# A decode block on one core: ScalarE's softmax work as a hardware loop, and one row of w_down per partition loaded ahead in three transfers

## The chip, the core and the metric

The kernel runs on one core of a Trainium2 chip. The metric is the device time of one execution in microseconds; before the change its median is 409.87 us over three runs (409.83 to 410.06). The profile shows one execution with its engines: PE (matmuls; its weight loads are shown as PEld), DVE (VectorE), ACT (ScalarE), POOL (GpSimd) and SP, which here only issues transfers. Behind SP's queue sixteen DMA engines move the bytes.

## What is computed

One token (B = S = 1) goes through an attention block over a cache of 65,536 keys and then through a gated feed-forward block. Everything is bf16 at the interface.

```python
D = 1024; Hq, Hkv, Sk, Dh = 32, 4, 65536, 128; F = 3584
q = (layernorm(x) @ wq).reshape(B, Sq, Hq, Dh).transpose(0, 2, 1, 3)
k, v = repeat(k_cache, 8, axis=1), repeat(v_cache, 8, axis=1)
p = softmax(einsum("bhqd,bhkd->bhqk", q, k) * Dh ** -0.5)
h = x + einsum("bhqk,bhkd->bhqd", p, v).transpose(0, 2, 1, 3).reshape(B, Sq, Hq * Dh) @ wo
n = layernorm(h)
h2 = h + (gelu(n @ w_gate) * (n @ w_up)) @ w_down
```

The caches are 2 x 64 MiB, the weights wq and wo 8 MiB each, w_gate, w_up and w_down 7 MiB each: 173 MB in all, every byte read once.

## The kernel before

**Staging.** All large inputs go through one buffer, `ring` (L162), of four slots of 32 KB per partition (4 MiB each). wq is read into slots 0 and 1. Then the caches are read in *half heads*: each of the four K/V heads is cut into two halves of 32,768 keys, so that `NT2` = 8 half heads t = 0 to 7 are worked on, one after the other. Of each, K comes as two transfers of 4 MiB, one to slot 2 and one to slot 3 (`k_load`, L211), and V as one of 8 MiB to slots 0 and 1 (`v_load`, L217). Behind the last half head wo takes slots 2 and 3, w_gate slots 0 and 1, w_up slots 2 and 3, and w_down slots 0 and 1 again.

**One half head.** DVE transposes K in four chunks (`k_chunk`), PE multiplies them with the query (L427), DVE transposes the scores into `sc` (`score`) and takes maxima. `softmax(t)` (L377) makes the maximum common to all partitions with two small PE operations and writes the negative bias `nb`. ACT then makes eight exponentials, one per query head, from `sc` into `pt`, each with a row sum into `lp` (L386). PE multiplies `pt` with V in 64 matmuls (L439), ACT copies the sum out of PSUM into `acc_sb` (`acc_copy`, L391), PE folds it with eight more (L448), and DVE copies the result to `o_raw` (`o_copy`).

**Who orders it.** The class `Flow` (L17) holds a list of operations for all engines; `op` (L31) finds which earlier operation each must wait for, and `issue` (L76) writes them out engine by engine in the order of the list, with semaphore waits. PE's part of the eight half heads alone is a hardware loop (`pe_loop`, L415), placed with `loop` (L66); ACT's and DVE's parts are written out eight times. PE counts its steps of a half head on the semaphore `s_step`, `STEPS` = 5 for each: 1 the transpose of the maxima, 2 the broadcast of the bias, 3 the first matmul with V, 4 the last matmul with V, 5 the last of the folding matmuls. Waits on this count are: `v_load(t)` on step 4 of half head t - 1, `score(t, 0)` on step 3 of t - 1, `softmax(t)` on steps 1 and 2, `acc_copy(t)` on step 4, `o_copy(t)` on step 5, and the load of w_gate on step 4 of half head 7 (L536).

**SP's queue** is served in order: wq twice, K(0) twice, then for each t V(t) and the two loads of K(t+1), then wo (L503), w_gate and w_up (L536), and w_down (L580 to L585) in four transfers.

**w_down.** Each partition gets 28 rows of 1,024 numbers (2 KB). The first 16 (`wa`, `FA` = 16) go to slot 0 as one transfer; the other 12 (`wb`, `FB` = 12) to slot 1 as three transfers of 8, 3 and 1 rows, each with its semaphore. At the end, outside the list, PE waits for each of these parts in turn and multiplies its rows (`down`, L590), eight matmuls a row, with some filling matmuls before the first and the second part (`stay_busy`, L596). DVE and ACT then copy the two halves of the result to `h2` (L607, L608), and SP stores it (L609).

**The end of the attention** (L454 to L478): from the biases DVE makes `mn` and `df`, ACT the factors `fa` that bring the two halves of a head to one scale, DVE the sums `lw` and `lsum`, PE adds them over partitions, and DVE weights `o_raw` with them. wo follows, then the second layer norm, w_gate, w_up and w_down.

Of the kernel before, what the change touches and what calls it, by code (L numbers as in the profile page):

```python
# [16 lines left out]
class Flow:  # L17
# [45 lines left out]
            self.readers[k] = []  # L63
        self.ops.append(dict(e=e, call=call, kw=kw, deps=sorted(deps), wait=wait, inc=inc, dma=dma))

    def loop(self, body):  # L66
        self.ops.append(dict(e="pe", call=body, loop=True, dma=False, inc=None))

    def dma(self, e, out, in_, r=(), w=(), after=(), wait=(), inc=None, sem=None):
        self.op(e, "dma_start", r, w, after, wait, inc, True, out=out, in_=in_)  # L70
# [38 lines left out]
def kernel(  # L109
# [76 lines left out]
    f = Flow(nc, tc)  # L186
    op = f.op
    from_dve, from_act, from_pool, s_v = [tc.alloc_semaphore("to_pe_%d" % i) for i in range(4)]
    s_qk, s_step = [tc.alloc_semaphore("from_pe_%d" % i) for i in range(2)]
    STEPS = 5  # L190
    k_sem = [tc.alloc_semaphore("k_landed_%d" % i) for i in range(DCH)]
    r_sem = [tc.alloc_semaphore("r_landed_%d" % i) for i in range(3)]

# [23 lines left out]
    def v_load(t):  # L217
        g, h = divmod(t, NH)
        n0 = h * CPH * CH
        f.dma("sp", slot(0, 2).rearrange("p (n d) -> p n d", d=Dh), v_v[g][:, n0:n0 + CPH * CH, :], after=["R0", "R1"],  # L220
              wait=[(s_step, STEPS * t - 1)] if t else [], inc=(s_v, 16))

    for p in range(PPH):
        k_load(0, p)
# [138 lines left out]

    def score(t, c):
        n = t * CPH + c
        op("dve", "transpose", w=["sc%d" % c], wait=[(s_qk, n + 1)] + ([(s_step, STEPS * t - 2)] if t and c == 0 else []),
           out=sc[:, c].rearrange("p n h s -> p (n h s)"), in_=bank[n % 2][:])
        if c >= CPH - 2:
            c0, i = (0, 0) if c == CPH - 2 else (c, 1)
            op("dve", "tensor_reduce", r=["sc%d" % x for x in range(c0, c + 1)], w=["mx%d" % i], out=mx[:, i, :],  # L370
               in_=sc[:, c0:c + 1].rearrange("p c n h s -> p h (c n) s"), axis=AX.XY, op=ALU.max)

    def o_copy(t):
        g, h = divmod(t, NH)
        op("dve", "tensor_copy", w=["o_raw%d" % t], wait=[(s_step, STEPS * t + 5)], out=o_raw[:, g, h, :], in_=o_ps)

    def softmax(t):  # L377
        g, h = divmod(t, NH)
        op("dve", "tensor_tensor", r=["mx0", "mx1"], inc=(from_dve, 1), out=mx1[:], in0=mx[:, 0, :], in1=mx[:, 1, :], op=ALU.max)
        op("dve", "tensor_reduce", w=["gm"], wait=[(s_step, STEPS * t + 1)], out=gm[:], in_=mxT_ps, axis=AX.X, op=ALU.max)  # L380
        op("dve", "tensor_scalar", r=["gm", "ident_f"], inc=(from_dve, 1), out=diag[:], in0=ident_f[0:rep, 0:rep], scalar1=gm[:, 0:1], scalar2=None,
           op0=ALU.mult)
        op("dve", "tensor_scalar", w=["nb%d" % t], wait=[(s_step, STEPS * t + 2)], out=nb[:, g, h, :], in0=bc_ps, scalar1=-scale, scalar2=None, op0=ALU.mult)
        for r in range(rep):
            last = r == rep - 1
            op("act", "activation", r=["nb%d" % t] if r == 0 else [], w=[] if last else ["lp%d_%d" % (t, r)],  # L386
               inc=(from_act, 1) if last else None,
               out=pt[:].rearrange("p c n h s -> p (c n) h s")[:, :, r, :], in_=sc[:].rearrange("p c n h s -> p (c n) h s")[:, :, r, :],
               func=ACT.Exp, bias=nb[:, g, h, r:r + 1], scale=scale, accum_out=lp[:, g, h, r:r + 1])

    def acc_copy(t):  # L391
        op("act", "copy", wait=[(s_step, STEPS * t + 4)], inc=(from_act, 1), out=acc_sb[:], in_=acc[:])

    for t in range(NT2):
        if t % NH == 0:
            make_qs(t // NH)
        for c in range(CPH):
            k_chunk(t, c)
            if c >= 1:
                score(t, c - 1)  # L400
            elif t:
                o_copy(t - 1)
        score(t, CPH - 1)
        v_load(t)
        if t + 1 < NT2:
            for p in range(PPH):
                k_load(t + 1, p)
        softmax(t)
        if t + 1 < NT2:
            acc_copy(t)  # L410

    def take(sem, n=1):
        nc.tensor.wait_ge(sem, n).then_inc(sem, -n)  # L413
# [1 line left out]
    def pe_loop():  # L415
        v_sb = slot(0, 2).rearrange("p (c s n d) -> p c s n d", c=CPH, s=NS, d=Dh)
        with nc.Fori(0, NT2, engines=(mybir.EngineType.PE,), head_slot={mybir.EngineType.PE: 0}):
            take(from_pool)
            with nc.tensor.Fori(0, PPH):
                for c in range(DCH):  # L420
                    take(from_dve)
                    for s in range(NS):
                        mv = ktb[:, c, s, :].bitcast(BF16).rearrange("p (n j b t) -> p n j b t", n=NN, j=2, t=2)
                        for jt in range(4):
                            J, u = divmod(jt, 2)
                            last = (s, jt) == (NS - 1, 3)
                            m = nc.tensor.matmul(bank[c][:], lhsT=qs[:, jt].rearrange("p s c -> p (s c)")[:, s * P:(s + 1) * P], rhs=mv[:, :, J, :, u], start=(s == 0 and jt == 0), stop=last)  # L427
                            if last:
                                m.then_inc(s_qk, 1)
            take(from_dve)  # L430
            nc.tensor.transpose(out=mxT_ps, in_=mx1[:], identity=ident_f[:]).then_inc(s_step, 1)  # L431
            take(from_dve)
            nc.tensor.matmul(bc_ps, lhsT=ones_f[0:rep, :], rhs=diag[:], start=True, stop=True).then_inc(s_step, 1)  # L433
            take(from_act)
            take(s_v, 16)
            for c in range(CPH):
                for n in range(NN):
                    q = n % 4
                    m = nc.tensor.matmul(acc[32 * q:32 * q + 32, :], lhsT=pt[:, c, n, :, :].rearrange("p h s -> p (h s)"),  # L439
                                         rhs=v_sb[:, c, :, n, :], start=(c == 0 and n < 4), stop=(c == CPH - 1 and n >= NN - 4),  # L440
                                         tile_position=(0, 32 * q))
                    if (c, n) == (0, 0):
                        m.then_inc(s_step, 1)
                    if (c, n) == (CPH - 1, NN - 1):
                        m.then_inc(s_step, 1)
            take(from_act)
            for u in range(NS):
                m = nc.tensor.matmul(o_ps, lhsT=acc_sb[:, u * Dh:(u + 1) * Dh], rhs=sel[:, u:SQ:NS], start=(u == 0), stop=(u == NS - 1))  # L448
            m.then_inc(s_step, 1)
# [5 lines left out]
    mn = sb("mn", [P, Hkv, rep])  # L455
    df = sb("df", [P, Hkv, NH, rep])
    fa = sb("fa", [P, Hkv, NH, rep])
    op("dve", "tensor_tensor", r=keys("nb"), w=["mn"], out=mn[:], in0=nb[:, :, 0, :], in1=nb[:, :, 1, :], op=ALU.min)
    for h in range(NH):
        op("dve", "tensor_tensor", r=["mn"], w=["df%d" % h], out=df[:, :, h, :], in0=mn[:], in1=nb[:, :, h, :], op=ALU.subtract)  # L460
    op("act", "activation", r=["df0", "df1"], w=["fa"], out=fa[:], in_=df[:], func=ACT.Exp)
# [1 line left out]
    op("dve", "tensor_tensor", r=["fa"], w=["lw"], out=lw[:], in0=lp[:], in1=fa[:], op=ALU.mult)  # L463
    lsum = sb("lsum", [P, Hkv, rep])
    op("dve", "tensor_tensor", r=["lw"], w=["lsum"], out=lsum[:], in0=lw[:, :, 0, :], in1=lw[:, :, 1, :], op=ALU.add)
    acc_copy(NT2 - 1)
    l_ps = bank[4][:, 0:Hq]
    op("pe", "matmul", r=["lsum", "ones_f"], w=["B4"], out=l_ps, lhsT=ones_f[:], rhs=lsum[:].rearrange("p g r -> p (g r)"), start=True, stop=True)
    rl = sb("rl", [P, Hkv, rep])
# [31 lines left out]
    at_ps = bank[6][:]  # L501
    wv = slot(2, 2).rearrange("p (c n) -> p c n", c=Hq)
    f.dma("sp", wv, A_wo.rearrange("(p c) n -> p c n", p=P), w=["R2", "R3"], wait=done, sem=r_sem[2])  # L503
    for c in range(Hq):
        for s in range(DS):
            q = 2 * (c % 2) + s
            op("pe", "matmul", r=["o2z", "R2", "R3"], w=["B6"], out=at_ps[32 * q:32 * q + 32, :], lhsT=o2z[:, c, :],
               rhs=wv[:, c, :].rearrange("k (p s c) -> k s p c", s=DS, c=C4)[:, s], start=(c < 2), stop=(c >= Hq - 2), tile_position=(0, 32 * q))
# [22 lines left out]
    def ffn_in(wmat, key, s0, b0):  # L531
# [1 line left out]
        bkeys = ["B%d" % (b0 + i) for i in range(2)]  # L533
        rk = ["R%d" % s0, "R%d" % (s0 + 1)]
        wv = slot(s0, 2)[:, 0:DC * F].rearrange("p (c n) -> p c n", c=DC)
        f.dma("sp", wv, wmat.rearrange("(p c) n -> p c n", p=P), w=rk, sem=r_sem[s0], wait=[(s_step, STEPS * NT2 - 1)])  # L536
        for ci in range(DC):
            wide_rows(banks, bkeys, hz, "xz", ci, f_blocks(wv[:, ci, :]), rk, ci == 0, ci == DC - 1)
        return rows_to_columns(banks, bkeys, key, "p (j e) -> p e j", j=32)
# [36 lines left out]
    FZ = 4  # L576
    wa = slot(0)[:, 0:FA * D].rearrange("p (e n) -> p e n", e=FA)
    wb = slot(1)[:, 0:FB * D].rearrange("p (e n) -> p e n", e=FB)
    wb_src = B_w_down[P * FA:F, :].rearrange("(p e) n -> p e n", p=P)
    parts = [(wa, 0, FA, f.dma("sp", wa, B_w_down[0:P * FA, :].rearrange("(p e) n -> p e n", p=P), after=["R0"], inc=(r_sem[0], 16)), r_sem[0])]  # L580
    e0 = 0
    for i, z in enumerate((FB - FZ, FZ - 1, 1)):
        part = wb[:, e0:e0 + z, :]
        s = (r_sem[1], k_sem[0], k_sem[1])[i]
        parts.append((part, FA + e0, z, f.dma("sp", part, wb_src[:, e0:e0 + z, :], after=["R1"] if i == 0 else [], inc=(s, 16)), s))  # L585
        e0 += z
# [12 lines left out]

    with tc.tile_critical(no_gpsimd_drain=True):  # L600
        for w_rows, a0, n, at, sem in parts:
            stay_busy({0: 4, FA: 4}.get(a0, 0))
            nc.tensor.wait_ge(sem, at)
            for e in range(n):
                down(actz[:, a0 + e, :], w_rows[:, e, :])
    h2 = sb("h2", [P, 2, OB], BF16)
# [33 lines left out]
```

## Time and profile before

| what | us |
|---|---|
| median of three runs | 409.87 |
| the profiled execution, its own time | 409.71 |
| its span | 407.8 |
| busy: PE / DVE / ACT / POOL | 234.8 / 202.5 / 39.5 / 19.2 |
| transfers of SP's queue, share of 16 engines' span | 98.5% |
| bytes read | 173.02 MB |
| one exponential on ACT / the eight of a half head | 0.49 / 3.9 |
| a copy to `acc_sb` on ACT | 0.59 |

The span runs from the first to the last thing that the profile shows; the profiled execution's own time is 1.9 us more. No engine but the transfers is busy for more than 58% of the span. ACT stands idle for 255.3 us in front of the exponentials, waiting for `nb`.

Two more kinds of record lie in the trace. Each transfer raises its semaphore in several events, one for each DMA engine as it finishes its share: they give the time at which each of the sixteen lands, though not which engine it is. And instructions are fetched by the same DMA engines, in blocks: five of 16 KB on queue 8, at 33.22, 358.00, 376.88, 401.08 and 404.62 us, and two of 8 KB on queue 14, at 99.83 and 143.25 us, in the span up to the last load.

### The profile page before, as it was taken

The numbers are of one execution on the slowest core, as the hardware profiler recorded it, in microseconds if no ns is written. First come the engines' busy times: TensorE is split into PE (matmuls) and PEld (weight loads), VectorE is DVE, ScalarE is ACT, GpSimd is POOL, SyncE is SP. The second block draws the span as 40 slices with busy tenths as digits, with TensorE's granted clock in tenths as the row PEclk, the third lists the DMA queues.
The fourth block names the chain that finished last, engine by engine and source line by source line (L and its number), as shares of the span: only waits on it lengthen the run. The fifth ranks groups of instructions, "written<-read, shape, count | busy, mean of one in ns | idle before, by whom it ended". The sixth has DMA issues, their size and how long they took to land. (4 is left out here: it accounts for less than half of the span.)

```text
span 407.8 us, 3909 instructions
## 1 busy us (share of the span) xinstructions
PE 234.8 (58%) x1645; PEld 105.8 (26%) x1647; DVE 202.5 (50%) x174; ACT 39.5 (10%) x141; POOL 19.2 (5%) x39
## 2 busy tenths in 40 slices
PE   0433855585577368734973686557465747365376
PEld 0211322232232133212321232223132223142324
DVE  1218860876089328924781687089508941010210
ACT  1000003000300300030003000300220021000000
POOL 4210000001000000010000001000000000012000
PEclk9955995599569967978796689689976976565668
DMA  8999999999999999999998999999999999999995
GB/s 344 427 421 452 415 460 411 460 418 412 453 460 418 411 425 488 418 408 421 476 437 376 453 424 444 421 460 418 411 453 466 418 418 424 452 440 435 399 413 220
DMA packets 4815, 173.12 MB, mean 424 GB/s; under 512 B 580, under 2 KB 584, under 8 KB 840
## 3 DMA queue, kind: packets, MB, share of 16 engines
q1 hardware_dynamic: 4760, 173.02, 98.5%
q8 instruction: 5, 0.08, 0.1%
q14 instruction: 2, 0.02, 0.0%
q10 hardware_dynamic: 48, 0.00, 0.0%
HBM read 173.02 MB, written 0.00 MB: 424 GB/s over the span
## 5 line engine op out<-in xcount | busy, mean ns | idle before, releaser
L95 DVE STREAM_TRANSPOSE ktb<-ring 128x4096 f32<-128x4096 f32 x32 | 141.1, 4418 | 83.4 <-DMA ring<-in_A_k_cache_dram 83.4
L427 PE MATMUL bank<-ktb,qs 128*128 128x512 bf16 x512 | 132.6, 418 | 61.3 <-PEq L413 61.3
L427 PEld LDWEIGHTS bank<-ktb,qs 128*128 128x128 bf16 x512 | 51.5, 104 | 139.2 <-issue 93.6
L439 PE MATMUL bank<-ring,pt 128*32 128x512 bf16 x512 | 46.3, 541 | 36.5 <-PEq L413 36.5
L95 ACT ACTIVATE pt<-sc,nb 128x256 bf16<-128x256 f32 x64 | 31.5, 494 | 255.3 <-DVE nb L95 255.3
L439 PEld LDWEIGHTS bank<-ring,pt 128*32 128x32 bf16 x512 | 19.4, 131 | 60.2 <-issue 57.3
L95 DVE STREAM_TRANSPOSE sc<-bank 128x512 f32<-128x512 f32 x32 | 22.2, 695 | 24.6 <-PE bank L427 24.6
L95 PE MATMUL bank<-ring,xz 128*32 128x512 bf16 (+1 forms) x192 | 19.2, 587 | 17.2 <-DMA ring<-in_B_w_gate_dram 5.2
L95 DVE TENSOR_REDUCE mx<-sc 128x8 f32<-128x1536 f32 (+1 forms) x16 | 19.5, 1219 | 0.5
L95 DVE STREAM_TRANSPOSE ktb<-bank 128x512 f32<-128x512 f32 (+1 forms) x6 | 4.0, 672 | 31.3 <-PE bank L95 30.9
L95 POOL COPY qs<-qsel 32x128 bf16<-32x128 bf16 x16 | 7.8, 490 | 231.4 <-PE bank L427 216.8
L95 PEld LDWEIGHTS bank<-ring,xz 128*32 128x32 bf16 x192 | 7.5, 141 | 26.9 <-issue 15.9
L95 ACT ACTIVATION_READ_ACCUMULATOR pt<-sc,nb 128x1 f32 x64 | 12.0, 187 | 0.0
L448 PE MATMUL bank<-sel,acc_sb 128*128 128x8 f32 x64 | 8.2, 255 | 6.2 <-PEq L413 6.2
L431 PE MATMUL bank<-ident_f,mx 128*8 128x128 f32 x8 | 2.2, 269 | 14.6 <-PEq L413 14.6
L448 PEld LDWEIGHTS bank<-sel,acc_sb 128*128 128x128 f32 x64 | 7.7, 191 | 10.0 <-issue 10.0
L95 PE MATMUL bank<-ring,ktb 128*32 128x512 bf16 x64 | 6.4, 586 | 5.9 <-DMA ring<-in_A_wo_dram 5.9
L95 ACT COPY acc_sb<-bank 128x512 f32<-128x512 f32 x8 | 4.7, 586 | 48.9 <-PE bank L439 48.9
L95 DVE TENSOR_TENSOR h_col<-bank,x_col 128x8 f32<-128x8 f32 x1 | 0.2, 167 | 14.8 <-PE bank L95 14.8
L95 PE MATMUL bank<-sel,ktb 128*128 128x16 f32 (+1 forms) x24 | 5.2, 356 | 3.5 <-DVE bank L95 2.7
L95 POOL MEMSET ktb<- 128x1024 bf16 (+2 forms) x3 | 3.5, 1164 | 75.8 <-PE bank L427 75.8
L433 PE MATMUL bank<-diag,ones_f 8*128 8x8 f32 x16 | 3.7, 299 | 5.7 <-PEq L413 5.7
(85 smaller groups left out, 60.9 us busy)
## 6 DMA issues: line engine op xcount, KB each, us to landing
ring<-in_A_k_cache_dram SPq DMA_DIRECT2D x16, 4096.0 KB, 24.9
ring<-in_A_wq_dram SPq DMA_DIRECT2D x2, 4096.0 KB, 16.7
ring<-in_B_w_gate_dram SPq DMA_DIRECT2D x1, 7168.0 KB, 26.9
ring<-in_B_w_up_dram SPq DMA_DIRECT2D x1, 7168.0 KB, 27.2
ring<-in_B_w_down_dram SPq DMA_DIRECT2D x1, 4096.0 KB, 20.4
ring<-in_B_w_down_dram SPq DMA_DIRECT2D x1, 2048.0 KB, 25.0
ring<-in_B_w_down_dram SPq DMA_DIRECT2D x1, 768.0 KB, 25.9
ring<-in_B_w_down_dram SPq DMA_DIRECT2D x1, 256.0 KB, 26.0
```

What stands on the lines that cost most here:

```text
L95: ins = getattr(self.eng[e], o["call"])(**o["kw"])
L427: m = nc.tensor.matmul(bank[c][:], lhsT=qs[:, jt].rearrange("p s c -> p (s c)")[:, s * P:(s + 1) * P], rhs=mv[:, :, J, :, u], start=(s == ...
L431: nc.tensor.transpose(out=mxT_ps, in_=mx1[:], identity=ident_f[:]).then_inc(s_step, 1)
L433: nc.tensor.matmul(bc_ps, lhsT=ones_f[0:rep, :], rhs=diag[:], start=True, stop=True).then_inc(s_step, 1)
L439: m = nc.tensor.matmul(acc[32 * q:32 * q + 32, :], lhsT=pt[:, c, n, :, :].rearrange("p h s -> p (h s)"), rhs=v_sb[:, c, :, n, :], start=(c ...
L448: m = nc.tensor.matmul(o_ps, lhsT=acc_sb[:, u * Dh:(u + 1) * Dh], rhs=sel[:, u:SQ:NS], start=(u == 0), stop=(u == NS - 1))
```

## The change

ACT's eight copies of exponentials and copy become one hardware loop over the half heads, `act_loop`. It is started for each half head by a semaphore of its own, `act_go`, which `softmax` raises when `nb` is written, and takes the count back by one each time. The operands `nb` and `lp` of a half head are addressed with the loop's register. For the copy to `acc_sb`, PE now raises a semaphore of its own too, `s_acc`, in place of step 4; so `STEPS` is 4 and step 4 is now the last of the folding matmuls. The loads of V and of w_gate and w_up wait for this step. `mn` waits for step 3 of the last half head. The last `acc_copy`, which stood behind `fa` in ACT's order, is now inside the loop and ahead of it.

The first of the 12 rows of `wb`, 256 KB over the 128 partitions, gets a tile of its own, `c_row`. It is loaded by three transfers, of the partitions 0 to 50, 51 to 114 and 115 to 127, which stand in SP's queue behind wo and ahead of w_gate and wait for nothing. The parts of `wb` behind it have 7, 3 and 1 rows. PE multiplies `c_row` at the head of the part of 7 rows, so the matmuls and their order stay as they were.

```diff
@@ -63,8 +63,8 @@
             self.readers[k] = []
         self.ops.append(dict(e=e, call=call, kw=kw, deps=sorted(deps), wait=wait, inc=inc, dma=dma))
 
-    def loop(self, body):
-        self.ops.append(dict(e="pe", call=body, loop=True, dma=False, inc=None))
+    def loop(self, body, e="pe"):
+        self.ops.append(dict(e=e, call=body, loop=True, dma=False, inc=None))
 
     def dma(self, e, out, in_, r=(), w=(), after=(), wait=(), inc=None, sem=None):
         self.op(e, "dma_start", r, w, after, wait, inc, True, out=out, in_=in_)
@@ -186,8 +186,9 @@
     f = Flow(nc, tc)
     op = f.op
     from_dve, from_act, from_pool, s_v = [tc.alloc_semaphore("to_pe_%d" % i) for i in range(4)]
-    s_qk, s_step = [tc.alloc_semaphore("from_pe_%d" % i) for i in range(2)]
-    STEPS = 5
+    s_qk, s_step, s_acc = [tc.alloc_semaphore("from_pe_%d" % i) for i in range(3)]
+    act_go = tc.alloc_semaphore("to_act")
+    STEPS = 4
     k_sem = [tc.alloc_semaphore("k_landed_%d" % i) for i in range(DCH)]
     r_sem = [tc.alloc_semaphore("r_landed_%d" % i) for i in range(3)]
 
@@ -218,7 +219,7 @@
         g, h = divmod(t, NH)
         n0 = h * CPH * CH
         f.dma("sp", slot(0, 2).rearrange("p (n d) -> p n d", d=Dh), v_v[g][:, n0:n0 + CPH * CH, :], after=["R0", "R1"],
-              wait=[(s_step, STEPS * t - 1)] if t else [], inc=(s_v, 16))
+              wait=[(s_step, STEPS * t)] if t else [], inc=(s_v, 16))
 
     for p in range(PPH):
         k_load(0, p)
@@ -363,7 +364,7 @@
 
     def score(t, c):
         n = t * CPH + c
-        op("dve", "transpose", w=["sc%d" % c], wait=[(s_qk, n + 1)] + ([(s_step, STEPS * t - 2)] if t and c == 0 else []),
+        op("dve", "transpose", w=["sc%d" % c], wait=[(s_qk, n + 1)] + ([(s_step, STEPS * t - 1)] if t and c == 0 else []),
            out=sc[:, c].rearrange("p n h s -> p (n h s)"), in_=bank[n % 2][:])
         if c >= CPH - 2:
             c0, i = (0, 0) if c == CPH - 2 else (c, 1)
@@ -372,7 +373,7 @@
 
     def o_copy(t):
         g, h = divmod(t, NH)
-        op("dve", "tensor_copy", w=["o_raw%d" % t], wait=[(s_step, STEPS * t + 5)], out=o_raw[:, g, h, :], in_=o_ps)
+        op("dve", "tensor_copy", w=["o_raw%d" % t], wait=[(s_step, STEPS * t + 4)], out=o_raw[:, g, h, :], in_=o_ps)
 
     def softmax(t):
         g, h = divmod(t, NH)
@@ -380,16 +381,21 @@
         op("dve", "tensor_reduce", w=["gm"], wait=[(s_step, STEPS * t + 1)], out=gm[:], in_=mxT_ps, axis=AX.X, op=ALU.max)
         op("dve", "tensor_scalar", r=["gm", "ident_f"], inc=(from_dve, 1), out=diag[:], in0=ident_f[0:rep, 0:rep], scalar1=gm[:, 0:1], scalar2=None,
            op0=ALU.mult)
-        op("dve", "tensor_scalar", w=["nb%d" % t], wait=[(s_step, STEPS * t + 2)], out=nb[:, g, h, :], in0=bc_ps, scalar1=-scale, scalar2=None, op0=ALU.mult)
-        for r in range(rep):
-            last = r == rep - 1
-            op("act", "activation", r=["nb%d" % t] if r == 0 else [], w=[] if last else ["lp%d_%d" % (t, r)],
-               inc=(from_act, 1) if last else None,
-               out=pt[:].rearrange("p c n h s -> p (c n) h s")[:, :, r, :], in_=sc[:].rearrange("p c n h s -> p (c n) h s")[:, :, r, :],
-               func=ACT.Exp, bias=nb[:, g, h, r:r + 1], scale=scale, accum_out=lp[:, g, h, r:r + 1])
-
-    def acc_copy(t):
-        op("act", "copy", wait=[(s_step, STEPS * t + 4)], inc=(from_act, 1), out=acc_sb[:], in_=acc[:])
+        op("dve", "tensor_scalar", wait=[(s_step, STEPS * t + 2)], inc=(act_go, 1), out=nb[:, g, h, :], in0=bc_ps, scalar1=-scale, scalar2=None, op0=ALU.mult)
+
+    def act_loop():
+        with nc.scalar.Fori(0, NT2) as t:
+            nc.scalar.wait_ge(act_go, 1).then_inc(act_go, -1)
+            nb_t = nb[:].rearrange("p g h r -> p (g h) r")[:, bass.ds(t, 1), :].rearrange("p t r -> p (t r)")
+            lp_t = lp[:].rearrange("p g h r -> p (g h) r")[:, bass.ds(t, 1), :].rearrange("p t r -> p (t r)")
+            for r in range(rep):
+                m = nc.scalar.activation(out=pt[:].rearrange("p c n h s -> p (c n) h s")[:, :, r, :], in_=sc[:].rearrange("p c n h s -> p (c n) h s")[:, :, r, :],
+                                         func=ACT.Exp, bias=nb_t[:, r:r + 1], scale=scale, accum_out=lp_t[:, r:r + 1])
+            m.then_inc(from_act, 1)
+            nc.scalar.wait_ge(s_acc, 1).then_inc(s_acc, -1)
+            nc.scalar.copy(out=acc_sb[:], in_=acc[:]).then_inc(from_act, 1)
+
+    f.loop(act_loop, "act")
 
     for t in range(NT2):
         if t % NH == 0:
@@ -406,8 +412,6 @@
             for p in range(PPH):
                 k_load(t + 1, p)
         softmax(t)
-        if t + 1 < NT2:
-            acc_copy(t)
 
     def take(sem, n=1):
         nc.tensor.wait_ge(sem, n).then_inc(sem, -n)
@@ -442,7 +446,7 @@
                     if (c, n) == (0, 0):
                         m.then_inc(s_step, 1)
                     if (c, n) == (CPH - 1, NN - 1):
-                        m.then_inc(s_step, 1)
+                        m.then_inc(s_acc, 1)
             take(from_act)
             for u in range(NS):
                 m = nc.tensor.matmul(o_ps, lhsT=acc_sb[:, u * Dh:(u + 1) * Dh], rhs=sel[:, u:SQ:NS], start=(u == 0), stop=(u == NS - 1))
@@ -455,7 +459,7 @@
     mn = sb("mn", [P, Hkv, rep])
     df = sb("df", [P, Hkv, NH, rep])
     fa = sb("fa", [P, Hkv, NH, rep])
-    op("dve", "tensor_tensor", r=keys("nb"), w=["mn"], out=mn[:], in0=nb[:, :, 0, :], in1=nb[:, :, 1, :], op=ALU.min)
+    op("dve", "tensor_tensor", w=["mn"], wait=[(s_step, STEPS * NT2 - 1)], out=mn[:], in0=nb[:, :, 0, :], in1=nb[:, :, 1, :], op=ALU.min)
     for h in range(NH):
         op("dve", "tensor_tensor", r=["mn"], w=["df%d" % h], out=df[:, :, h, :], in0=mn[:], in1=nb[:, :, h, :], op=ALU.subtract)
     op("act", "activation", r=["df0", "df1"], w=["fa"], out=fa[:], in_=df[:], func=ACT.Exp)
@@ -463,7 +467,6 @@
     op("dve", "tensor_tensor", r=["fa"], w=["lw"], out=lw[:], in0=lp[:], in1=fa[:], op=ALU.mult)
     lsum = sb("lsum", [P, Hkv, rep])
     op("dve", "tensor_tensor", r=["lw"], w=["lsum"], out=lsum[:], in0=lw[:, :, 0, :], in1=lw[:, :, 1, :], op=ALU.add)
-    acc_copy(NT2 - 1)
     l_ps = bank[4][:, 0:Hq]
     op("pe", "matmul", r=["lsum", "ones_f"], w=["B4"], out=l_ps, lhsT=ones_f[:], rhs=lsum[:].rearrange("p g r -> p (g r)"), start=True, stop=True)
     rl = sb("rl", [P, Hkv, rep])
@@ -501,6 +504,10 @@
     at_ps = bank[6][:]
     wv = slot(2, 2).rearrange("p (c n) -> p c n", c=Hq)
     f.dma("sp", wv, A_wo.rearrange("(p c) n -> p c n", p=P), w=["R2", "R3"], wait=done, sem=r_sem[2])
+    wb_src = B_w_down[P * FA:F, :].rearrange("(p e) n -> p e n", p=P)
+    c_row = sb("c_row", [P, 1, D], BF16)
+    for p0, p1 in ((0, 51), (51, 115), (115, P)):
+        f.dma("sp", c_row[p0:p1], wb_src[p0:p1, 0:1, :], inc=(r_sem[1], 16))
     for c in range(Hq):
         for s in range(DS):
             q = 2 * (c % 2) + s
@@ -533,7 +540,7 @@
         bkeys = ["B%d" % (b0 + i) for i in range(2)]
         rk = ["R%d" % s0, "R%d" % (s0 + 1)]
         wv = slot(s0, 2)[:, 0:DC * F].rearrange("p (c n) -> p c n", c=DC)
-        f.dma("sp", wv, wmat.rearrange("(p c) n -> p c n", p=P), w=rk, sem=r_sem[s0], wait=[(s_step, STEPS * NT2 - 1)])
+        f.dma("sp", wv, wmat.rearrange("(p c) n -> p c n", p=P), w=rk, sem=r_sem[s0], wait=[(s_step, STEPS * NT2)])
         for ci in range(DC):
             wide_rows(banks, bkeys, hz, "xz", ci, f_blocks(wv[:, ci, :]), rk, ci == 0, ci == DC - 1)
         return rows_to_columns(banks, bkeys, key, "p (j e) -> p e j", j=32)
@@ -576,10 +583,9 @@
     FZ = 4
     wa = slot(0)[:, 0:FA * D].rearrange("p (e n) -> p e n", e=FA)
     wb = slot(1)[:, 0:FB * D].rearrange("p (e n) -> p e n", e=FB)
-    wb_src = B_w_down[P * FA:F, :].rearrange("(p e) n -> p e n", p=P)
     parts = [(wa, 0, FA, f.dma("sp", wa, B_w_down[0:P * FA, :].rearrange("(p e) n -> p e n", p=P), after=["R0"], inc=(r_sem[0], 16)), r_sem[0])]
-    e0 = 0
-    for i, z in enumerate((FB - FZ, FZ - 1, 1)):
+    e0 = 1
+    for i, z in enumerate((FB - FZ - 1, FZ - 1, 1)):
         part = wb[:, e0:e0 + z, :]
         s = (r_sem[1], k_sem[0], k_sem[1])[i]
         parts.append((part, FA + e0, z, f.dma("sp", part, wb_src[:, e0:e0 + z, :], after=["R1"] if i == 0 else [], inc=(s, 16)), s))
@@ -599,8 +605,10 @@
 
     with tc.tile_critical(no_gpsimd_drain=True):
         for w_rows, a0, n, at, sem in parts:
-            stay_busy({0: 4, FA: 4}.get(a0, 0))
+            stay_busy({0: 4, FA + 1: 4}.get(a0, 0))
             nc.tensor.wait_ge(sem, at)
+            if a0 == FA + 1:
+                down(actz[:, FA, :], c_row[:, 0, :])
             for e in range(n):
                 down(actz[:, a0 + e, :], w_rows[:, e, :])
     h2 = sb("h2", [P, 2, OB], BF16)

```

## Prediction

> **What bounds the kernel.** I read the page's slices and queues first, then the chain of waits, then the timeline around the places that the change touches. The slices and queues:
>
> ```profile
> PE   0433855585577368734973686557465747365376
> DVE  1218860876089328924781687089508941010210
> DMA  8999999999999999999998999999999999999995
> ...
> q1 hardware_dynamic: 4760, 173.02, 98.5%
> q8 instruction: 5, 0.08, 0.1%
> q14 instruction: 2, 0.02, 0.0%
> ...
> HBM read 173.02 MB, written 0.00 MB: 424 GB/s over the span
> ```
>
> The DMA row is full from the second slice to the last but one, while PE and DVE have holes everywhere. So this is one stream of 173.02 MB, and what counts is when its last byte lands and what follows it. In the trace's DMA records each of the sixteen engines takes 1.209 us per row of 32 KB, without a gap: 27.1 GB/s. The timeline of the end:
>
> ```profile
> 402.38 0.62 PE L593 MATMUL bank<-ring,ktb 128*32 128x128 bf16 x30 [0.53 <-DMA ring<-in_B_w_down_dram]
> 404.23 0.35 PEld L593 LDWEIGHTS bank<-ring,ktb 128*32 128x32 bf16 x24 [0.22 <-DMA ring<-in_B_w_down_dram]
> 404.85 0.12 PEld L593 LDWEIGHTS bank<-ring,ktb 128*32 128x32 bf16 x8 [0.28 <-DMA ring<-in_B_w_down_dram]
> 405.34 0.28 DVE L607 CAST h<-bank 64x128 bf16<-64x128 f32 x1 [9.89 <-PEq L600]
> 405.71 0.35 SPq L609 DMA_DIRECT2D out_dram<-h  x1
> ```
>
> PE waits for w_down at each part. The last row's transfer lands at 404.81, its eight matmuls start at 404.85, the copy at 405.34, the store at 405.71. After the last landing come 407.8 - 404.81 = 2.99 us that the change leaves alone. (The chain of waits holds only that last copy, 0.28 us, so it says no more.)
>
> **The sixteen engines do not end together.** The landing events of that last transfer, after the first (402.97), are 0, 0.12, 0.12, 0.13, 0.17, 0.20, 0.27, 0.35, 0.38, 0.50, 0.79, 1.32, 1.54, 1.68, 1.70 and 1.84 us. The transfer that lands at 32.55 has all sixteen within 0.41. Each late engine appears right after an instruction fetch: the 16 KB at 33.22 turn one from about 0.3 to 1.81 late, the 8 KB at 99.83 one from 0.33 to 1.31, at 143.25 one from 0.11 to 0.78, and those at 358.00, 376.88 and 401.08 three more by about 1.5 each. They never catch up, since all engines are always full. The end is thus that of the engine hit at 33.22, and more rows for an engine cost nothing until it passes that one.
>
> **The change, part by part.**
>
> *1. The loads that wait for a later step.* V(t+1) and w_gate now wait for the last folding matmul, not the last V matmul:
>
> ```profile
> 303.33 0.33 SPq L95 DMA_DIRECT2D ring<-in_A_v_cache_dram  x1
> 303.34 0.58 ACT L95 COPY acc_sb<-bank 128x512 f32<-128x512 f32 x1 [5.79 <-PE bank L439]
> 304.07 1.03 PE L448 MATMUL bank<-sel,acc_sb 128*128 128x8 f32 x8 [0.78 <-PEq L413]
> 305.43 4.45 DVE L95 STREAM_TRANSPOSE ktb<-ring 128x4096 f32<-128x4096 f32 x1 [11.96 <-DMA ring<-in_A_k_cache_dram]
> ...
> 343.84 0.33 SPq L95 DMA_DIRECT2D ring<-in_B_w_gate_dram  x1
> 344.57 1.03 PE L448 MATMUL bank<-sel,acc_sb 128*128 128x8 f32 x8 [0.78 <-PEq L413]
> ...
> 353.95 6.44 PE L95 MATMUL bank<-ring,ktb 128*32 128x512 bf16 x64 [5.89 <-DMA ring<-in_A_wo_dram]
> ```
>
> That is 304.07 + 1.03 - 303.33 = 1.77 us later. Cover: V is issued while the second K transfer still has to run. From the issue to the first engine that ends that K it is 7.8 us at the tightest half head (111.58 to 119.39), 9.9 at this one; w_gate has 8.1 (343.84 to 351.97, wo's first landing). The first issue of the kernel took 1.0 us to its first byte (1.01 to 2.03), so 6.8 is left and 5.0 after the new wait. Behind V in SP's queue stand K loads that wait for later PE work anyway; behind w_gate stands w_up, which waits for wo's matmuls (360.48). Cost 0; with the cover gone, 1.77 us a half head, 14 in all.
>
> *2. ACT's loop.* Exponentials are the same 8 of 0.49 us. Added: a wait and a branch a half head, a register for two operands, perhaps a table load (one of 1.28 us at 1.76 before). Not shown before; bounds 0 and 8 x 0.51 + 1.28 = 5.4 us (each exponential as long again, a table load each time). I take 1: the branch falls into the 27 us in which ACT waits for `nb`. Cover: 5.0 us from part 1; on PE the next K matmuls start 2.7 us after the fold at the tightest half head (113.3 to 116.0), and K's loads have 25 us from issue to landing against 9.7 of transfer. Cost 0; even the upper bound leaves 0.4 us a half head of V late, 3 in all.
>
> *3. The end of the attention.* `mn` now waits for PE's first V matmul (337.90, was 333.57); behind it on DVE stand `df`, `lw`, `lsum` and all up to `o2_bf`. `fa` comes after ACT's copy, 343.84 + 0.59 + 0.24 = 344.7, then `lw` and `lsum`, 0.23 + 0.19: about 345.2. PE reaches their sum at 345.43 anyway. The chain up to POOL's copy ends at 348.67 and wo lands at 353.82: 5.1 us of cover. Cost 0.
>
> *4. Three more issues on SP*, 0.33 us each, between wo (329.99) and w_gate (343.84), where SP waits 13 us: cost 0. The 256 KB leave the tail and run ahead of w_gate: w_gate lands about 0.4 us later, w_down is issued later, with 10 us of w_up still running (377.01 to 387.72). PE has the same matmuls after each of the last parts, which land as far apart as before. Cost 0.
>
> *5. How the 128 rows are dealt.* Here the end can move. Before, `c_row`'s bytes were 8 rows of 2 KB per engine. Transfers in the trace are dealt in equal shares: 128 rows raise a semaphore sixteen times, x's 32 rows too, and the store's 4 rows once at 406.17 and four times at 406.85 to 406.90, as if four engines worked. Equal shares of 64 rows are 16 x 4, of 13 rows 13 x 1, of 51 only 3 x 17 (or 1 x 51). So three engines would get 17 + 4 + 1 = 22 rows, ten get 5, three get 4. A 2 KB row costs 0.079 us (the last transfer, 8 rows, lands 0.63 after the one before), a semaphore event 0.009, and a row taken out of a longer one saves 2 KB at 27.1 GB/s, 0.076. Three engines: 22 x 0.079 + 3 x 0.009 - 8 x 0.076 = **+1.15 us**; ten: 5 x 0.079 + 2 x 0.009 - 0.61 = **-0.20**; three: -0.28. The last engine comes 0.20 to 0.28 earlier, if it is not among the loaded three and none of them passes it: those may be up to 0.5 late now (1.65 against 1.84 - 0.20). If instead the rows are spread over all sixteen, nothing moves: 0. The other bound, all 51 on one engine, is 56 rows there (68 with all 13 as well), +3.8 to +4.8 us; I leave it outside the range, since the store's rows are the nearest case and were dealt as widely as they go.
>
> [...]
>
> Sum: 0 + 0 + 0 + 0 - 0.20 = -0.2 us on the span (407.8 to 407.6) and on the profiled 409.71. The median of the runs stands 0.16 above that execution, so 409.87 - 0.2 = 409.67, rounded **409.7 us**.
>
> **The rivals.**
>
> *A late engine is among the loaded three (slower).* Its price is 1.15 us on an engine that is 1.84, 1.70, 1.68, 1.54 or 1.32 late: the end moves to 411.0, 410.9, 410.9, 410.7 or 410.5. It decides from 0.69 late on, and passes 0.2% from 1.51. For it: no record numbers the engines, and blind draws of three hit one of the four latest in 1 - 220/560 = 61%. Against: followed back by their spacing, four late ones (143.25, 358.00, 376.88, 401.08) began the kernel within about 0.1 us of each other, so they may be neighbours; a block of four misses three given places in 10 of 13 positions, and the engine of 33.22 in 13 of 16, 62%. I take half.
>
> *ACT's loop fetches its code again at each turn (slower).* A fetch of 8 KB made an engine 0.67 to 0.98 later. Seven turns back on one early engine, 0.3 + 7 x 0.67 = 5.0 against 1.84: +3.1, 413.0; it decides from the third. Against: PE goes through its longer loop eight times between 34 and 358 us without one fetch on queue 8. [...]
>
> *The change does not do what it says:* the rows go evenly to sixteen engines: 409.87, part of "same". *Faster by more than 0.2%:* with all engines ending at the mean of the sixteen (0.69 late) the end would come 1.15 earlier, 408.7; for that nothing in parts 1 to 5 is enough.
>
> **How the numbers follow.** 0.2%, 0.82 us, is about what a measurement of this kernel can tell from no change. Even dealing 0.18; three loaded engines early enough 0.36; a late one among them 0.34; ACT fetching again 0.07; faster 0.05. The first two are my forecast, 409.7 to 409.9, chance 0.54: same 0.54. Slower 0.34 + 0.07 = 0.41 (the hits below 0.82 us weigh little, as do unpriced waits on the other side), faster 0.05. The range reaches from 409.4, a little more than 0.28 gained, to 411.1, past 409.87 + 1.15; out stay ACT's fetches and the fast case, 0.12. The forecast's own range is 409.4 to 410.0.
>
> **What would show it.** The landing events of the transfers behind `c_row`: three engines about 1.15 later than before against the rest, last landing near 404.6 if right, near 406 if a late engine carries more. V and w_gate issued 1.8 to 3 us later with the DMA row still full: parts 1 and 2; a gap there would refute them. Queue 14's fetches: two or fewer, or eight and more in the second rival. PE's and DVE's groups keep their times. A gap in the DMA row, a last landing that doesn't move, or an end more than 2.99 us behind it would make me wrong.

## The result, and the profile after

The change made the kernel slower: 411.27 us, the median of seven runs (410.94 to 411.84), against 409.94 (409.74 to 410.06) for the kernel before, run beside it. The ratio is 1.0034, with a 95% interval of 1.0023 to 1.0045. The profiled execution took 410.94 us, 1.23 more than the one of before, with a span of 408.9.

From the page of the changed kernel, the slices, the queues and one group:

```profile
DMA  8999999999999999999999998999999999999995
...
q1 hardware_dynamic: 4920, 173.02, 98.6%
q8 instruction: 5, 0.08, 0.1%
...
q14 instruction: 1, 0.01, 0.0%
HBM read 173.02 MB, written 0.00 MB: 423 GB/s over the span
...
L392 ACT ACT_TABLE_LOAD x8 | 10.3, 1283 | 249.1 <-ACTq L388 249.1
```

The same bytes, the same full DMA row. Queue 14 has one fetch less, the one at 143.25, which was thus ACT's; and ACT loads its table in each of the eight turns.

The timeline around a V load and the w_gate load (start, duration, engine, what it does, idle time before):

```profile
295.03 0.51 ACT L392 ACTIVATE pt<-sc,nb 128x256 bf16<-128x256 f32 x1
...
306.38 0.33 SPq L95 DMA_DIRECT2D ring<-in_A_v_cache_dram  x1
...
346.05 0.36 SPq L95 DMA_DIRECT2D ring<-in_B_w_gate_dram  x1
348.76 0.32 POOL L95 COPY ktb<-o_bf 128x32 bf16<-128x32 bf16 x1 [19.16 <-DVE o_bf L95]
```

V is issued 3.05 us later than before (303.33), the 1.77 of the new wait and the 1.28 of the table load; w_gate 2.2 later; the attention's last step 0.4 later (348.35). None of it leaves a hole in the transfers.

The end, in the timeline:

```profile
403.29 0.30 PE L599 MATMUL bank<-c_row,ktb 128*32 128x128 bf16 x8
403.41 0.50 PE L599 MATMUL bank<-ring,ktb 128*32 128x128 bf16 x22
405.07 1.12 PE L599 MATMUL bank<-ring,ktb 128*32 128x128 bf16 x66 [1.16 <-issue]
406.37 0.28 DVE L615 CAST h<-bank 64x128 bf16<-64x128 f32 x1 [9.64 <-PEq L606]
406.74 0.29 SPq L617 DMA_DIRECT2D out_dram<-h  x1
```

The landing events of the last transfer complete the picture. The first of the sixteen lands at 404.11 (402.97 before), then 0.01, 0.05, 0.09, 0.11, 0.12, 0.17, 0.25, 1.11, 1.21, 1.46, 1.51, 1.55, 1.56, 1.57 and 1.60 us later (the last was 1.84 before). So the sum of the profiled difference is: first landing +1.14, spread of the sixteen -0.24, from the last landing (405.71) to the copy 0.66 against 0.53, +0.13, from the copy to the end of the span +0.01, outside the span +0.19 (the spans are 407.85 and 408.89): 1.23 us.

All sixteen engines are late, not three. Where they lose it is seen in one window around the row's transfers. Its columns are the stretch, its length, then each engine's busy time, the granted clock, the DMA share and GB/s. First before, then after:

```profile
349.00:357.00 8.00, 3.05 (x32) 1.33 (x36) 0.00 (x0) 0.00 (x0) 0.00 (x0) 0.50 1.07 461
```

```profile
349.00:357.00 8.00, 2.09 (x21) 0.88 (x25) 0.00 (x0) 0.00 (x0) 0.09 (x1) 0.50 1.08 393
```

The share that the engines are busy is the same (a row counts whole where it starts, so it can pass 1), the bytes are 15% fewer: they work all the time, but slower. The DMA records say which rows: the first row of w_gate, 57,344 bytes, takes 3.10 to 3.31 us on eleven engines, where it took 2.12 before. Half of the 2 KB rows of `c_row` take over 0.12 us, instead of the 0.084 that such a row takes in w_down's last transfer before. Below, *loss* is the sum over the records in a stretch of duration minus the usual duration for that size, divided by sixteen. It comes from the one profiled execution of each kernel. From 348 to 358 us it is 0.00 before and **1.26 us** after.

### The profile page after: what moved, and what is told of

The parts are those of the page before. It is cut to its first block, busy times and chain, and to the rows that moved or that the text cites. A ratio compares the mean times of both kernels' runs of the same rounds, so it can differ in the third digit from the quotient of the medians.

```text
span 408.9 us, 4026 instructions
## 1 busy us (share of the span) xinstructions
PE 230.0 (56%) x1647; PEld 104.0 (25%) x1647; DVE 202.5 (50%) x174; ACT 48.4 (12%) x148; POOL 19.3 (5%) x39
## 5 line engine op out<-in xcount | busy, mean ns | idle before, releaser
L431 PE MATMUL bank<-ktb,qs 128*128 128x512 bf16 x512 | 129.9, 412 | 53.8 <-PEq L417 53.8
L443 PE MATMUL bank<-ring,pt 128*32 128x512 bf16 x512 | 45.0, 528 | 48.2 <-PEq L417 48.2
L392 ACT ACTIVATION_READ_ACCUMULATOR pt<-sc,nb x64 | 12.0, 187 | 0.0
```

The costliest lines, as they stand in the source:

```text
L392: m = nc.scalar.activation(out=pt[:].rearrange("p c n h s -> p (c n) h s")[:, :, r, :], in_=sc[:].rearrange("p c n h s -> p (c n) h s")[:, ...
```

## The experiments

Times are against the kernel before, run beside them: 409.89 for e1 to e4, 409.91 for f1 to f4, 409.86 for g1 to g3.

### Which half of the change

*e1: the loop alone.* `c_row` and its transfers are taken out; w_down is loaded as before.

> ACT's loop alone; w_down is loaded as before. Theory A (the 1.26 us that each DMA engine loses between 348 and 356 us comes from the row's three transfers): no change, -0.2 to +0.2 us against the kernel before, last landing about 404.8. Theory B (the loop's later issues of V and w_gate cost it): +0.9 us or more, and rows of 57,344 bytes longer than 2.12 us again.

409.90 us, ratio 1.0000 (0.9990 to 1.0009). Loss 0.00, last landing 404.80. The loop with its eight table loads and the later issues of V and w_gate cost nothing that the runs show. Theory B falls.

*e2: the row alone.* ACT's work is written out as before.

> The row's three transfers alone; ACT's work written out as before. Theory A: +1.0 to +1.4 us, with the first rows of w_gate at 3.3 us instead of 2.12. Theory B: -0.3 to 0 us, the gain of the dealing that the prediction had.

411.74 us, ratio 1.0046 (1.0029 to 1.0062): the row's transfers carry it, with a loss of 1.34. That is 1.85 us more than before, past the 1.0 to 1.4 that I had expected, and 0.47 above the whole change; the intervals of the two overlap. The landing events of its profiled execution show what may add to it: at 334 us one engine is 0.80 late, which ACT's fetch at 144.49 left there and which the whole change doesn't have; at the end the last engine is 2.16 late, not 1.60. The 0.80, the 1.15 of a loaded engine and the 0.20 that the unloaded ones gain, both estimates of part 5, make 2.15. So the engine of ACT's fetch is most likely one of the three that the transfer of 51 partitions loads, and the loop, which is worth nothing by itself, would make room on it. No record numbers the engines, so this is argued, not shown.

### Uneven shares, number of transfers, or place

*e3: one transfer,* `((0, P),)` for the three. *e4: three transfers with even shares,*

```diff
-    for p0, p1 in ((0, 51), (51, 115), (115, P)):
+    for p0, p1 in ((0, 48), (48, 112), (112, P)):
```

> The changed kernel with the row loaded by one transfer of 128 partitions, 8 rows of 2 KB on each of sixteen engines. Theory A (the three engines' 17 rows each slow all the others): no loss of rate, 0 to +0.2 us against the kernel before. Theory C (any 2 KB rows of w_down ahead of w_gate slow the stream): +0.9 us or more.

> The changed kernel with the row split into 48, 64 and 16 partitions: three transfers still, but 3 + 4 + 1 = 8 rows on each of sixteen engines, at the same odd places of the partitions. Theory A: no loss of rate, 0 to +0.2 us. Theory C': three transfers, or rows that an engine does not write in the usual 128-partition pattern, cost it: +0.9 us or more and rows of w_gate over 2.12 us.

e3: 410.24 us, ratio 1.0009 (0.9999 to 1.0018), loss 0.03. e4: 411.34 us, ratio 1.0035 (1.0023 to 1.0048), loss 0.92. The window of e3, then of e4:

```profile
349.00:357.00 8.00, 3.03 (x34) 1.28 (x36) 0.26 (x2) 0.00 (x0) 0.32 (x1) 0.54 1.12 479
```

```profile
349.00:357.00 8.00, 2.08 (x20) 0.89 (x24) 0.00 (x0) 0.00 (x0) 0.00 (x0) 0.50 1.02 386
```

The same row at the same place of the queue costs no rate in one transfer, and in three with even shares most of what the changed kernel lost. So my theory A, the three overloaded engines, is wrong; left are the number of transfers and the way in which a transfer of fewer than 128 partitions is dealt.

*f1: three transfers of all partitions,* cut by columns. *f2: two of 64 partitions,* `((0, 64), (64, P))`.

```diff
-    for p0, p1 in ((0, 51), (51, 115), (115, P)):
-        f.dma("sp", c_row[p0:p1], wb_src[p0:p1, 0:1, :], inc=(r_sem[1], 16))
+    for n0, n1 in ((0, 408), (408, 920), (920, D)):
+        f.dma("sp", c_row[:, :, n0:n1], wb_src[:, 0:1, n0:n1], inc=(r_sem[1], 16))
```

> The changed kernel with the row split by columns (408, 512 and 104 numbers) into three transfers of all 128 partitions. Theory P (the rate falls because rows are dealt to other engines than in a 128-partition transfer): no loss of rate, and the time of the single transfer (e3), 0 to +0.4 us. Theory N (three small transfers in a row cost it): loss of 1 us or more, +1.2 us or more.

> The changed kernel with the row in two transfers of 64 partitions, 4 rows on each engine twice. Theory P: rows of w_gate at 2.5 us and more, a loss of 0.5 to 1.2 us of each engine's time, +0.8 to +1.5 us. Theory that only odd boundaries (48, 51, 115) matter: no loss, 0 to +0.4 us.

f1: loss 0.05, 410.47 us (ratio 1.0016, 1.0006 to 1.0026). f2: loss 1.49, 411.59 us (1.0041, 1.0026 to 1.0055), w_gate rows up to 3.45. The window of f1, then of f2:

```profile
349.00:357.00 8.00, 2.79 (x28) 1.24 (x32) 0.20 (x2) 0.00 (x0) 0.32 (x1) 0.50 1.17 486
```

```profile
349.00:357.00 8.00, 1.42 (x20) 0.60 (x22) 0.26 (x2) 0.00 (x0) 0.32 (x1) 0.55 1.06 374
```

The pieces of f1 are under 2 KB, a size for which the kernel before has no usual duration, so the large rows alone are the safer comparison: they lose 0.02 in f1 and 1.17 in f2. Neither three transfers nor odd boundaries are what it takes to lose the rate. The loss of f2 was above the 0.5 to 1.2 that I had expected.

Without a loss the row ahead still does not pay: e3 is 0.35 us above the kernel before (its interval just includes no change) and f1 0.56, both more than I had expected. Part of this may lie at the end of PE, below.

*f3: the three transfers at the head of the queue,* between wq and the first K, with a semaphore of their own. *f4: at the tail,* the last row of `wb` in 48, 64 and 16 partitions, nothing behind it, nothing moved ahead.

> The changed kernel with the three transfers (51, 64, 13) at the head of SP's queue, behind wq and ahead of the first K, where the sixteen engines land within 0.4 us of each other. Theory P alone: the same loss there, 1 to 1.3 us, rows of K longer than 1.215 us, +1 to +1.4 us. Theory L (it needs engines that are 1.2 to 1.8 us apart): little loss, under 0.4 us, and -0.2 to +0.5 us.

> ACT's loop alone, w_down as before, but its last row, the last transfer of all, split into 48, 64 and 16 partitions: 8 rows on each engine and no large rows behind. Theory P: the 2 KB rows take 0.13 us and more instead of 0.084 and the end moves by about 0.4 us. If the loss needs large rows beside the small ones: 0.084 us each, -0.1 to +0.2 us.

f3: 411.21 us (1.0030, 1.0018 to 1.0043); the loss goes with the transfers, about 1.15 from 18 to 30 us, 0.00 at the old place. The engines are within 0.4 us of each other there, so theory L falls. f4: 410.78 us (1.0024, 1.0014 to 1.0034); loss 0.41 at the end, 2 KB rows up to 0.18, last landing 405.70 instead of 404.81. That the end moved by 0.9 where the mean loss is 0.41 I can't take apart; it may be that the loss falls on some engines more than on others, but no record says which engine a row ran on.

### Whose partitions an engine writes

The next two kernels rest on a supposition of mine that no record shows: the engines are dealt the partitions of a 128-partition transfer so that each writes a set of its own, and a smaller transfer can make them write into each other's sets (theory P'). g1 is meant to keep to the sets and g2 to leave them; all else is held equal. Both start from e3 and add eight small transfers into an unused tile, of 8 partitions each, four apart; both read the same rows; only the target partitions differ, by four. I took each small transfer to go to the same eight engines, one row each: an estimate from the changed kernel, where 13 partitions raised 13 events. The added lines, without the tile, its semaphore and PE's wait for it, which are the same in both; the second `f.dma` is that of g2 in place of the first:

```diff
+    for b in (0, 1, 2, 3, 32, 33, 34, 35):
+        f.dma("sp", d_row[b + 0:b + 0 + 29:4], wb_src[b:b + 29:4, 0:1, :], inc=(d_sem, 16))      # g1
+        f.dma("sp", d_row[b + 4:b + 4 + 29:4], wb_src[b:b + 29:4, 0:1, :], inc=(d_sem, 16))      # g2
```

> The kernel of e3 (the row in one transfer) with eight more transfers into an unused tile, each of 8 partitions four apart (0, 4, ... 28 and so on): together they hold each of the partitions 0 to 63 once. [...] Theory P': no loss of rate, under 0.2 us; the eight engines get 8 rows more, 0.7 to 0.8 us, so the time is that of e3 to 0.8 us above it. Theory that any transfer of fewer than 128 partitions costs: loss of 0.5 us and more.

> [...] Theory P' (what costs is an engine writing partitions that another engine writes at the same time): a loss of rate of 0.4 us or more, rows of w_gate at 2.5 us and more, time 0.3 to 1.2 us above g1. If the target partitions do not matter (HBM side, number of engines): the same as g1 within 0.2 us.

g1: loss 0.11, 410.74 us (1.0017, 1.0007 to 1.0026). g2: loss **1.09**, 411.36 us (1.0037, 1.0023 to 1.0051), w_gate rows up to 3.35 (2.50 in g1). The window of g1, then of g2:

```profile
349.00:357.00 8.00, 3.13 (x32) 1.40 (x36) 0.00 (x0) 0.00 (x0) 0.00 (x0) 0.50 1.10 460
```

```profile
349.00:357.00 8.00, 2.48 (x24) 1.05 (x28) 0.00 (x0) 0.00 (x0) 0.12 (x1) 0.50 1.05 388
```

Moving the targets by four partitions turns a loss of 0.11 into 1.09, and every run of g2 (from 411.18) is slower than every run of g1 (to 411.08). The rows read, their size and the number of transfers are the same, so it is the targets. That the rate falls when an engine writes partitions that in a full transfer are another's would fit these losses; but since no record numbers the engines, which engine writes which partition was not shown.

The kernels with a loss of 0.9 us or more have medians of 411.21 to 411.74 us. Those with the row in full transfers (e3, f1, g1 and g3 below) have a loss of 0.11 at most and medians of 410.24 to 410.74.

### The end of PE

In e3 the last transfer lands at 404.89, 0.08 later than before, and yet the copy comes at 405.98, 0.64 later. Its timeline:

```profile
402.62 0.50 PE L599 MATMUL bank<-ring,ktb 128*32 128x128 bf16 x22
404.68 1.13 PE L599 MATMUL bank<-ring,ktb 128*32 128x128 bf16 x66 [1.56 <-issue]
405.98 0.28 DVE L615 CAST h<-bank 64x128 bf16<-64x128 f32 x1 [9.90 <-PEq L606]
```

PE stands for 1.56 us with 66 matmuls to go, waiting for nothing that a semaphore shows. It is so in each kernel, with 62 to 66 left, and always after a fetch on queue 8 that fires near the end of `wa`'s 128 matmuls or shortly behind it: record 401.08 to 402.16 and resumed at 403.50 before, 402.73 to 403.82 and 405.07 after, 402.18 to 403.26 and 404.68 in e3. In the timeline of before it is this line, which the prediction's lines of the end do not include:

```profile
403.50 1.65 PE L593 MATMUL bank<-ring,ktb 128*32 128x128 bf16 x66 [0.49 <-issue]
```

There the 66 matmuls waited for the last landings anyway. With a row moved ahead, less time lies between the landing of `wa` and the last landing (6.7 us in e3, 7.4 before), so PE can be later with its last block than the data. It isn't always: from the last landing to the copy it is 1.09 us in e3, 1.04 in e2 and 0.66 in the changed kernel, but in f1 and g1 0.53, as before.

*g3* starts from e3, multiplies the loaded row ahead of `wa` and drops the four filling matmuls behind it:

```diff
-            stay_busy({0: 4, FA + 1: 4}.get(a0, 0))
+            stay_busy({0: 4}.get(a0, 0))
+            if a0 == 0:
+                nc.tensor.wait_ge(r_sem[1], 32)
+                down(actz[:, FA, :], c_row[:, 0, :])
             nc.tensor.wait_ge(sem, at)
-            if a0 == FA + 1:
-                down(actz[:, FA, :], c_row[:, 0, :])
```

> The kernel of e3 with PE multiplying the loaded row first, ahead of wa, and without the four filling matmuls ahead of the part of 7 rows. Theory S (e3's end is late since PE waits, about 66 matmuls from its end, for a block of instructions that it asks for only when it is through wa, which lands later now): the fetch on queue 8 fires earlier than at 402.18, PE resumes earlier than 404.68, and the copy comes 0.3 us or more earlier; -0.3 us against e3. If PE waits for a transfer instead: no change.

In its profiled execution the fetch fires at 401.98, PE resumes at 404.33, the copy comes at 405.58, 0.4 earlier than in e3. But the median is 410.27 (1.0013, 1.0003 to 1.0023), no better than e3's. And f1, which has PE's work in the order of e3, fetches at 401.97 and resumes at 404.37 in its own execution. So what moved between the two executions of e3 and g3 may be chance: theory S is neither shown nor refuted, and no gain in time is shown.

## Why the prediction was wrong, point by point

**Right: the bound and the shares.** The stream bounds the kernel. The semaphore of `c_row` rose in 66 events, which is wq and the part of 7 rows with sixteen each, 16 for 64 partitions, 3 and 13 single ones for the others and two at the issue. In equal shares that is 3 x 17, 16 x 4 and 13 x 1, as part 5 had it. Eight engines end 1.11 to 1.60 behind the first: two were late at 334 us, three fetches came later, and three more are by this count the loaded ones. They fitted, as the forecast case had it. That the three with 17 rows each are also among the 13 of the last transfer, 22 rows in all, and that they lie together at one end of the sixteen, as the 10 of 13 positions suppose, no run shows; the changed kernel shows the 66 events and the eight late landings. The spread of the last transfer fell by 0.24, but that is not the 0.20 of the forecast, by which the first engine would have gained as much as the last; f3, with the same dealing, has a spread of 1.86.

**Wrong: part 5's price of a row.** It took 0.079 us for 2 KB from the last transfer of w_down, and nothing for all other rows. That row is one of a 128-partition transfer. In transfers of 51, 64 and 13 partitions the rows cost a loss of 1.26 us, the mean of the sixteen engines. This is the step that failed: 1.26 not seen less 0.20 gained is 1.06, against a first landing 1.14 and a last landing 0.90 later. No rival had it: all asked how much each engine gets, none where it writes. Even two transfers of 64 partitions (f2) had 2 KB rows of up to 0.36 us instead of 0.084, and the large rows beside them slowed down too, from 2.12 to up to 3.45 us.

**Wrong, smaller: part 4's "PE has the same matmuls after each of the last parts. Cost 0".** It overlooked PE's stand behind its fetch, which the timeline of before has as 0.49 us of "issue" in front of 66 matmuls. Covered then, it costs 0.13 in the changed kernel's profile, some 0.56 in e3's (1.09 us from landing to copy against 0.53) and nothing in f1's. So the time behind the last landing was not left alone: 3.18 us against 3.04 before (2.99 in the prediction, from a rounded span).

**The rivals.** A late engine among the loaded three came out at 410.5 to 411.0. That is close to what was measured, by luck: the reason is another. e2 is most likely a case in which it holds, and there it adds to the loss. ACT's loop fetched nothing again. The range ended at 411.1, past the dearest hit on a late engine, and was 0.2 short; the one dearer rival, ACT's fetches at 413.0, had been left outside.

**Parts 1 to 3** held: 3.05 and 2.2 us later issues, a table load a turn (the upper bound's guess), 0.4 us in the attention's end, and e1 shows no cost of theirs.

## What to carry to other kernels

In a kernel that lives on its stream, split transfers by columns or rows of all 128 partitions, not by partitions: here one 256 KB row cut at partition 64 cost a loss of 1.49 us (f2), cut by columns 0.05 (f1), against 0.03 in one transfer (e3). Before cutting a transfer by partitions, try where its targets may lie: the same eight small transfers lost 0.11 us in g1 and 1.09 in g2, four partitions higher. And where work is moved out of a tail, look at what else the tail was covering: "issue" time in front of the last matmuls becomes a cost when nothing longer covers it, as in e3's profile: 1.09 us from the last landing to the copy instead of 0.53.

## What had not been expected of the hardware

The loss reaches the large rows that run beside the small ones: in the changed kernel eleven engines took 3.10 to 3.31 us for their first w_gate row. It seems to outlast them a little: there the last small row ends at 354.66 us, and the w_gate row that starts then still takes 2.34 us, against 2.12 for those from 355.25 on. In f2 it ends at 355.91, and a w_gate row from then on takes 2.28. Why it spreads to all sixteen, and why it lasts, is open; it wasn't tried.

In the kernel before, an engine that was held up by one instruction fetch stayed late to the end, by 0.67 to 1.5 us for 8 or 16 KB. The last of the sixteen landings, which the fetch at 33.22 us put back, was 1.81 us behind the first in the transfer from 41.84 us on and 1.84 in the one that ends at 404.81, 371.6 us after the fetch.

PE resumed 1.25 to 1.54 us after the record of its fetch ended, and stood 0.5 to 1.6 us at the same place of its code in each profile.
